# A fused attention and MLP kernel: 64-row matmuls made 128 rows high, transposes in other PSUM banks, weight blocks requested earlier

## The chip, the cores and the metric

The kernel runs on one core of a Trainium2 chip. The metric is the device time of one execution, in microseconds (us).

## What is computed

Three parts follow each other. Batch is 4, heads 8, sequence 576, head dimension 64, 128 features, model width 512.

```python
def _attn_ref(q, k, v, w_phi):            # (4, 8, 576, 64), w_phi (64, 128)
    def phi(x):
        proj = np.einsum('bhsd,df->bhsf', x, w_phi)
        proj = proj - np.max(np.abs(proj), axis=-1, keepdims=True)
        return np.concatenate([np.exp(proj), np.exp(-proj)], axis=-1)
    q_p, k_p = (phi(q), phi(k))
    kv = np.einsum('bhsf,bhsd->bhfd', k_p, v)
    z = np.sum(k_p, axis=2)
    num = np.einsum('bhsf,bhfd->bhsd', q_p, kv)
    den = np.einsum('bhsf,bhf->bhs', q_p, z)[..., None] + 1e-06
    return num / den
def _moe_ref(x, w_ch1, w_ch2):            # x (4, 576, 512), w_ch1 (512, 2048), w_ch2 (2048, 512)
    u = x + np.real(np.fft.fft(np.fft.fft(x, axis=1), axis=2))
    un = layer_norm(u)
    return u + np.maximum(un @ w_ch1, 0.0) @ w_ch2
def _moe2_ref(x, g_ln, w_ch1, w_ch2):
    return x + np.maximum((layer_norm(x) * g_ln) @ w_ch1, 0.0) @ w_ch2
```

`layer_norm` stands for the mean and variance over the last axis written out in the reference. The MLP weights come in double precision and the kernel makes single-precision numbers of them.

## The kernel before

**First stage: attention and DFT, to about 320 us.** The 32 heads are worked in 16 units of two heads. 576 tokens are four tiles of 128 and a rest of 64. The rest of q and the rest of k share one tile, "mix": q in rows 0 to 63, k in rows 64 to 127. For each unit `project` (L116) multiplies the tiles with w_phi (pp, in PSUM), VectorE takes the largest magnitude (mx) and subtracts it (pm). `k_exp` (L134) has ScalarE make both exponentials of k (ek); for mix it takes rows 64 to 127 alone. `kv` (L143) sums over keys (pk): five tiles, two heads, two signs, each matmul in two instructions; the last tile uses rows 64 to 127 alone (L148). `q_exp` (L160) transposes the q tiles on TensorE, the four full ones into pt (named ptq in the profile), the 64 rows of mix into ptc (L162), and ScalarE makes the exponentials eq from both (L168, L169). `num` (L172) multiplies eq with the sums z (px), and VectorE divides (L188 to L201). The DFT of the real attention output is done by symmetry: `fold` (L206) adds or subtracts mirrored halves, `seq_stage` (L233) transforms along the sequence (pb), `dim_stage` (L271) along the model width (pd). A last matmul in `dim_stage` (L285) takes the rows nyq, four of them used, times alt, a row of alternating signs; both are 64 rows high.

**PSUM.** All banks come from three tags (L48): p has two banks and holds pp, ptc and in the second stage ph; t has two for pt and ptx; n has four for pk, px, pb, pd and acc.

**Second stage: the two MLPs.** Weights come in 64 blocks of 512 KB, eight to a group of 512 hidden columns. `fetch` (L314) requests one block (wraw) on the queue of SyncE into one of two raw buffers (`RAW = 2`, L28); `to_float` (L329 to L343) makes single precision of it on ScalarE and VectorE (wm), with the last read of the raw buffer at L342; `decode` (L345) calls `fetch` and `to_float` and splits the result into a high and a low part (wh, wl). `mm1` (L418) makes ph and from it hh and hl on ScalarE and VectorE, `mm2` (L436) makes acc, and VectorE adds it to the result.

**Order.** The program order is written out: `rounds` (L559) for the units, `pieces` (L527) for decode and DFT steps of a round, `side` (L478) for steps between `mm1` and `mm2`. The framework then works out the order on each engine by its own timeline simulation (L657). Decode steps stand in rounds 2 to 17 for the first group (L532) and at fixed places of the group before for the others (L493 to L498):

```python
        for k in range(8):
            side.setdefault((0, 2 + k // 4, 2 * (k % 4)), []).append(partial(decode, 0, 1, k))
        for p in range(1, 7):
            for k in range(8):
                at = (p, k // 2, 1 + 4 * (k % 2))
                side.setdefault(at, []).append(partial(decode, (p + 1) // 4, (p + 1) % 4, k))
```

Of the kernel before, what the change touches and what calls it, by code (L numbers as in the profile page):

```python
# [10 lines left out]
F32 = mybir.dt.float32  # L11
F32R = mybir.dt.float32r
I32 = mybir.dt.int32
U32 = mybir.dt.uint32
AF = mybir.ActivationFunctionType
# [3 lines left out]
B, H, S, D = 4, 8, 576, 64  # L19
F = 128  # L20
DM = H * D
NE = DM // 2 + 2
# [9 lines left out]
def fused_kernel(ctx, tc, qk_c, v_c, w_phi, w1s, w2s, g_ln, cs_c, cd_c, perm_c, out):  # L32
    nc = tc.nc
    P = 128
# [7 lines left out]
    dpool = dft_stack.enter_context(tc.tile_pool(name="dft", bufs=1))  # L42
    att_stack = ExitStack()
    apool = att_stack.enter_context(tc.tile_pool(name="atk", bufs=1, side="right"))
    bpool = att_stack.enter_context(tc.tile_pool(name="atq", bufs=1))

    def ps_tile(tag, shape, name):
        return psum.tile(shape, F32, tag=tag, bufs={"p": 2, "t": 2, "n": 4}[tag], name=name)  # L48
# [5 lines left out]
    ident = perm  # L54
# [5 lines left out]

    cs = dpool.tile([P, 3, 2, 2, NS], F32R, name="cs")
    cd = dpool.tile([P, 2, 2, 2, NE], F32R, name="cd")
    alt = dpool.tile([64, NE], F32R, name="alt")
    wbd = apool.tile([P, 2, F], F32, name="wbd")

    def load_consts():
# [7 lines left out]
    def load_dft_consts():  # L74
        nc.sync.dma_start(perm, perm_c)
        for x, c in ((cs, cs_c), (cd, cd_c[0:P])):
            x = x.rearrange("p a b c e -> p (a b c e)")
            follow(x[:, 0:1], 0)
            nc.gpsimd.dma_start(x, c)
        nc.gpsimd.dma_start(alt, cd_c[P : P + 64, 0:NE])  # L80

    def late_consts():
        nc.sync.dma_start(gcol, g_ln.rearrange("(k p) -> p k", p=P))
# [12 lines left out]
    st = [dict() for _ in range(NUNIT)]  # L96
# [19 lines left out]
    def project(u, name):  # L116
# [14 lines left out]
        nc.vector.tensor_tensor(out=t, in0=pp, in1=mx.unsqueeze(2).to_broadcast([P, 2 * n, F]), op=ALU.subtract)  # L131
        st[u]["pm", name] = t

    def k_exp(u, name):  # L134
        t = st[u]["pm", name]
        n = 1 if name == "mix" else 2
        r = slice(64, P) if name == "mix" else slice(0, P)
        e = apool.tile([P, 2 * n, 2, F], F32, tag=f"ek{n}", bufs=2, name="ek")
        for sgn in range(2):
            nc.scalar.activation(e[r, :, sgn], t[r], AF.Exp, scale=1.0 - 2.0 * sgn)  # L140
        st[u]["ek", name] = e

    def kv(u):  # L143
        pk = ps_tile("n", [P, 4, D + 1], "pk")
        first = True
        for t in range(5):
            e = st[u]["ek", ("k0", "k1", "mix")[t // 2]]
            r = slice(64, P) if t == 4 else slice(0, P)  # L148
            for j in range(2):
                for sgn in range(2):  # L150
                    nc.tensor.matmul(  # L151
                        pk[:, 2 * j + sgn, :], e[r, 2 * (t % 2) + j, sgn], st[u]["v"][r, t, j],
                        start=first, stop=(t == 4), skip_group_check=True,
                    )
                    first = False
        z = bpool.tile([P, 4, D + 1], F32, tag="z", bufs=2, name="z")
        nc.scalar.copy(z, pk)
        st[u]["z"] = z

    def q_exp(u, j):  # L160
        ptc = ps_tile("p", [P, 64], "ptc")
        nc.tensor.transpose(ptc, st[u]["pm", "mix"][0:64, j, :], ident[0:64, 0:64])  # L162
        pt = ps_tile("t", [P, 4, P], "ptq")
        for t in range(4):
            nc.tensor.transpose(pt[:, t, :], st[u]["pm", f"q{t // 2}"][:, 2 * (t % 2) + j, :], ident)  # L165
        e = bpool.tile([P, 2, S], F32, tag="eq", bufs=2, name="eq")
        for sgn in range(2):
            nc.scalar.activation(e[:, sgn, 512:S], ptc, AF.Exp, scale=1.0 - 2.0 * sgn)  # L168
            nc.scalar.activation(e[:, sgn, 0:512], pt.rearrange("p t s -> p (t s)"), AF.Exp, scale=1.0 - 2.0 * sgn)  # L169
        st[u]["eq", j] = e  # L170

# [59 lines left out]
    nyq = []  # L231

    def seq_stage(b, w):  # L233
        xs = dst[b].pop(("x", w))
        bh = dpool.tile([P, 2, 2 * P], F32R, tag="bh", bufs=2, name="bh")
        bl = dpool.tile([P, 2, 2 * P], F32R, tag="bl", bufs=2, name="bl")
        if b % 2 == 0:
            mixed[w] = [dpool.tile([P, 2, P], F32R, tag=f"b{x}{w}", bufs=1, name=f"b{x}{w}") for x in "pq"]
        ch, cl = mixed[w]
        if w == 0:  # L240
            if not nyq:
                nyq.append(dpool.tile([64, 3 * P], F32R, name="nyq"))
                nc.vector.memset(f32(nyq[0]), 0.0)
        r = slice(64 * (b % 2), 64 * (b % 2) + 64)
        for m in range(3 - w):
            pb = ps_tile("n", [P if m < 2 else 2, NS], "pb")
            mm = []
            for kk in range(3):
                for cc in range(2):
                    if m < 2:  # L250
                        c = slice(m * P, (m + 1) * P)
                        mm.append((pb, xs[:, kk, c], cs[:, kk, w, cc]))
                        if kk < 2 and cc == 0:
                            mm.append((pb, xs[:, 3 + kk, c], cs[:, kk, w, cc]))
                    elif kk < 2:
                        mm.append((pb, xs[:, kk : kk + 4 : 3, 256], cs[:, kk, w, cc]))
                    else:
                        mm.append((pb[0:1], xs[:, kk, 256:257], cs[:, kk, w, cc]))
            for n, (o, a, c) in enumerate(mm):
                nc.tensor.matmul(o, a, c, start=(n == 0), stop=(n == len(mm) - 1), skip_group_check=(m == 2))  # L260
            if m < 2:
                parts = ((bh[:, m], bl[:, m]), (ch[:, m, r], cl[:, m, r]))
            else:
                rc = slice(2 * P + r.start, 2 * P + r.stop)
                parts = [(nyq[0][0:2, x], nyq[0][32:34, x]) for x in (slice(0, 2 * P), rc)]
            for (oh, ol), src in zip(parts, (pb[:, 0 : 2 * P], pb[:, 2 * P : NS])):
                nc.scalar.copy(oh, src)
                nc.vector.tensor_tensor(out=ol, in0=src, in1=f32(oh), op=ALU.subtract)
        dst[b]["b", w] = (bh, bl)
# [31 lines left out]


    weights = {}
    wpools = {}

    def group_tiles(layer, g):
# [7 lines left out]
    def fetch(layer, g, n):  # L314
        w, i = divmod(n, 4)
        src = w1s[layer] if w == 0 else w2s[layer]
        r = slice(i * P, (i + 1) * P) if w == 0 else slice(g * 512 + i * P, g * 512 + (i + 1) * P)
        c = slice(g * 1024, (g + 1) * 1024) if w == 0 else slice(0, 1024)
        raw = wpool.tile([P, WB, 2], I32, tag="wraw", bufs=RAW, name="wraw")
        if layer == 0 and g == 0 and n < RAW:  # L320
            follow(f32(raw[:, 0, 0:1]), 1)
        nc.sync.dma_start(raw.rearrange("p f t -> p (f t)"), src.bitcast(I32)[r, c])
        return raw

    def to_float(raw):

# [18 lines left out]
    def decode(layer, g, n):  # L345
        if n == 0:
            group_tiles(layer, g)
        w, i = divmod(n, 4)
        wh, wl = weights[layer, g][w]
        raw = fetch(layer, g, n)  # L350
        m = to_float(raw)
        if layer == 1 and w == 0:

            nc.scalar.activation(wh[:, i], f32(m), AF.Copy, scale=gcol[:, i : i + 1])
            nc.vector.scalar_tensor_tensor(
                out=wl[:, i], in0=f32(m), scalar=gcol[:, i : i + 1], in1=f32(wh[:, i]),
                op0=ALU.mult, op1=ALU.subtract,
            )
        else:
            nc.scalar.copy(wh[:, i], f32(m))  # L360
            nc.vector.tensor_tensor(out=wl[:, i], in0=f32(m), in1=f32(wh[:, i]), op=ALU.subtract)
# [112 lines left out]
    def moe(last_dft):  # L474
# [3 lines left out]
        side = {}  # L478
# [11 lines left out]
        side.setdefault((0, 1, 2), []).append(partial(prepare, 0, 2))  # L490
        side.setdefault((0, 1, 7), []).append(partial(prepare, 0, 3))
        side.setdefault((0, 2, 7), []).append(partial(prepare, 0, 4))
        for k in range(8):  # L493
            side.setdefault((0, 2 + k // 4, 2 * (k % 4)), []).append(partial(decode, 0, 1, k))
        for p in range(1, 7):
            for k in range(8):
                at = (p, k // 2, 1 + 4 * (k % 2))
                side.setdefault(at, []).append(partial(decode, (p + 1) // 4, (p + 1) % 4, k))  # L498

        for layer, g, c in steps:  # L500
            p = 4 * layer + g
# [15 lines left out]


    nc.vector.memset(ub[0][:, 0], 0.0)
    warm = ps_tile("n", [P, DM], "warm")  # L520
    for n in range(2):
        nc.tensor.matmul(warm, ub[0][:, 0, 0:P], ub[0][:, 0], start=True, stop=True)
# [4 lines left out]
    def at(step, f, *a):  # L527
        pieces.setdefault(step, []).append((f, a))

    wpools[0] = wpool  # L530
    xpools[0] = xpool
    for n, step in enumerate((2, 3, 4, 7, 8, 11, 15, 17)):  # L532
        at(step, decode, 0, 0, n)
    at(9, prepare_norm, 0)
    at(12, prepare_tiles, 0, 0, (0, 1))
# [28 lines left out]
    for i in range(NUNIT + 2):  # L564
        for name, ahead in rounds:
            u = i + ahead
# [27 lines left out]
def _constants():  # L594
# [7 lines left out]
    e = np.arange(NE)  # L602
    ang = 2 * np.pi * ((d[:, :, None] * e[None, None, :]) % DM) / DM
    live = (e <= DM // 2).astype(np.float64)
    cd = np.stack([np.stack(_split(f(ang) * live), axis=2) for f in (np.cos, np.sin)], axis=1)
    cd = cd.reshape(128, -1)
    last = np.zeros((64, cd.shape[1]), np.float32)
    last[[0, 1, 32, 33], :NE] = np.where(e % 2 == 0, 1.0, -1.0) * live
    perm = np.eye(128, dtype=np.float32)
    return (  # L610
# [54 lines left out]
```

## Time and profile before

| | |
|---|---|
| median of 3 runs | 1109.78 us (1109.66 to 1110.68) |
| the profiled execution, in all | 1109.95 us |
| its span, first to last instruction | 1108.2 us |
| granted TensorE clock, mean share | 0.994 |
| TensorE (PE) busy | 1086.3 us |
| weight loads (PEld) busy | 927.9 us |
| VectorE (DVE) busy | 615.0 us |
| ScalarE (ACT) busy | 340.5 us |
| GpSimd (POOL) busy | 45.3 us |

Busy time of an engine is the time in which at least one of its instructions runs. Matmuls are pipelined and overlap: one starts before the one ahead has ended, so the spacing of their starts tells more than their durations. In the rows a shape such as 64*128 64x65 is rows*columns of the weights in the array, then partitions x elements of the moving operand. In a timeline row the first number is the start of a merged group in us, the second its length from the first start to the last end, xN the number of instructions, and what stands in brackets is the idle time of the engine before it and what ended it.

### The profile page before, as it was taken

How to read it: one execution, taken by the hardware profiler on the slowest of the kernel's cores; microseconds unless marked ns; L12 is line 12 of the kernel's file. 1: busy time of each engine (PE TensorE's matmuls, PEld its weight loads, DVE VectorE, ACT ScalarE, POOL GpSimd, SP SyncE). 2: the span in 40 equal slices, each digit the busy share in tenths (PEclk: the TensorE clock that was granted, in tenths of full speed). 3: DMA queues.
4: the chain of work that ended last, by engine and by line, in shares of the span. 5: the costliest groups of instructions: out<-in, count | busy, mean ns of one | idle time of the engine just before them, and what ended most of it. 6: DMA issues, size and time to landing. Idle time of an engine off the chain costs nothing.

```text
span 1108.2 us, 14381 instructions
## 1 busy us (share of the span) xinstructions
PE 1086.3 (98%) x5806; PEld 927.9 (84%) x5806; DVE 615.0 (55%) x1315; ACT 340.5 (31%) x682; POOL 45.3 (4%) x53
## 2 busy tenths in 40 slices
PE   9899999999999999999999999999999999999996
PEld 7789989999788888888888788888878888888885
DVE  5897586774879476238327755762383264222131
ACT  4545454454435131113113343521231132011110
POOL 1000020300210000000000000000000000000010
PEclk9899999999999999999999999999999999999998
DMA  7452121110003122003101300220031011000111
GB/s 257 144 161 77 46 60 42 57 46 1 1 1 114 39 76 76 1 1 114 39 1 50 103 1 1 64 89 1 1 115 38 1 39 38 1 1 10 48 48 67
DMA packets 19755, 57.26 MB, mean 52 GB/s; under 512 B 2728, under 2 KB 3432, under 8 KB 19432
## 3 DMA queue, kind: packets, MB, share of 16 engines
q1 hardware_dynamic: 18536, 51.01, 14.3%
q0 software_dynamic: 1008, 5.19, 1.3%
q8 instruction: 46, 0.75, 0.3%
q14 instruction: 21, 0.17, 0.1%
q10 hardware_dynamic: 144, 0.13, 0.0%
HBM read 51.60 MB, written 4.72 MB: 51 GB/s over the span
## 4 chain that ended last, share of the span: by engine, by line
PE 86%; DVE 8%; DMA 4%; ACT 2%; issue 1%; POOLq 0%; POOL 0%; DVEq 0%; SPq 0%; ACTq 0%
PE acc L443 33%; PE ph L427 32%; PE pk L151 5%; PE px L181 5%; PE pp L121 5%; DMA wraw<-in_moe_w_ch 4%; PE pb L260 2%; PE ptq L165 1%; PE ptx L409 1%; PE pd L287 1%; DVE wm L342 1%; DVE wm L337 1%; DVE xx L215 1%; DVE wm L334 0%; DVE hl L431 0%
## 5 line engine op out<-in xcount | busy, mean ns | idle before, releaser
L427 PE MATMUL ph<-xth,wh 128*128 128x512 f32 (+1 forms) x640 | 236.2, 369 | 0.7 <-ACT xth L411 0.7
L427 PE MATMUL ph<-xtl,wh 128*128 128x512 f32 (+1 forms) x640 | 235.8, 368 | 0.0
L427 PE MATMUL ph<-xth,wl 128*128 128x512 f32 (+1 forms) x640 | 235.7, 368 | 0.0
L431 DVE SCALAR_TENSOR_TENSOR hl<-ph,hh 128x512 fp32r<-128x512 f32 (+1 forms) x160 | 101.5, 634 | 232.7 <-ACT hh L430 232.4
L430 ACT ACTIVATE hh<-ph 128x512 fp32r<-128x512 f32 (+1 forms) x160 | 88.4, 554 | 461.6 <-PE ph L427 456.4
L443 PE MATMUL acc<-wl,hh 128*128 128x512 f32 x576 | 224.2, 390 | 0.0
L443 PE MATMUL acc<-wh,hh 128*128 128x512 f32 x576 | 221.2, 391 | 2.5 <-ACT hh L430 2.5
L443 PE MATMUL acc<-wh,hl 128*128 128x512 f32 x576 | 195.3, 390 | 0.0
L427 PEld LDWEIGHTS ph<-xth,wh 128*128 128x128 f32 x640 | 120.4, 188 | 21.8 <-ACT xth L411 0.9
L427 PEld LDWEIGHTS ph<-xtl,wh 128*128 128x128 f32 x640 | 120.5, 188 | 20.7
L427 PEld LDWEIGHTS ph<-xth,wl 128*128 128x128 f32 x640 | 120.6, 188 | 20.0
L445 DVE TENSOR_TENSOR u<-acc,u 128x512 f32<-128x512 f32 x128 | 81.2, 682 | 94.3 <-PE acc L443 94.1
L443 PEld LDWEIGHTS acc<-wh,hh 128*128 128x128 f32 x576 | 108.1, 188 | 25.4 <-ACT hh L430 3.6
L443 PEld LDWEIGHTS acc<-wl,hh 128*128 128x128 f32 x576 | 108.2, 188 | 22.1
L443 PEld LDWEIGHTS acc<-wh,hl 128*128 128x128 f32 x576 | 107.1, 188 | 21.2
L121 PE MATMUL pp<-wbd,qk 128*128 128x256 f32 x288 | 80.2, 398 | 3.2 <-ACT eq L168 1.9
L151 PEld LDWEIGHTS pk<-vv,ek 128*128 128x128 f32 (+1 forms) x640 | 77.6, 191 | 5.2 <-ACT ek L140 1.8
L151 PE MATMUL pk<-vv,ek 128*128 128x65 f32 (+1 forms) x640 | 80.1, 273 | 0.8 <-ACT ek L140 0.6
L181 PEld LDWEIGHTS px<-z,eq 128*128 128x128 f32 (+1 forms) x640 | 76.3, 186 | 3.9 <-issue 0.3
L181 PE MATMUL px<-z,eq 128*128 128x65 f32 (+1 forms) x640 | 76.1, 268 | 0.0
L125 DVE TENSOR_REDUCE mx<-pp 128x4 f32<-128x512 f32 (+1 forms) x80 | 50.5, 631 | 45.5 <-PE pp L121 44.8
L140 ACT ACTIVATE ek<-pm 128x512 f32<-128x512 f32 (+1 forms) x96 | 48.2, 551 | 44.5 <-DVE pm L131 44.2
(100 smaller groups left out, 954.2 us busy)
## 6 DMA issues: line engine op xcount, KB each, us to landing
wraw<-in_moe_w_ch SPq DMA_DIRECT2D x64, 512.0 KB
vv<-in_v SPq DMA_DIRECT2D x16, 325.0 KB
qk<-in_qk SPq DMA_DIRECT2D x15, 320.0 KB
qk<-in_qk SPq DMA_DIRECT2D x16, 256.0 KB
out<-u SPq DMA_DIRECT2D x8, 256.0 KB
cs<-c_seq POOLq DMA_DIRECT2D x1, 1920.0 KB, 10.3
cd<-c_dim POOLq DMA_DIRECT2D x1, 1032.0 KB, 13.0
out<-uc SPq DMA_DIRECT2D x4, 126.0 KB
```

The source lines that it names most:

```text
L121: nc.tensor.matmul(pp[:, 2 * i : 2 * i + 2, :], qk[:, KT[name] + i], wbd.rearrange("p h f -> p (h f)"), start=True, stop=True)
L125: nc.vector.tensor_reduce(out=mx, in_=pp, op=ALU.max, axis=AX.X, apply_absolute_value=True)
L140: nc.scalar.activation(e[r, :, sgn], t[r], AF.Exp, scale=1.0 - 2.0 * sgn)
L151: nc.tensor.matmul(pk[:, 2 * j + sgn, :], e[r, 2 * (t % 2) + j, sgn], st[u]["v"][r, t, j], start=first, stop=(t == 4), skip_group_check=True,)
L165: nc.tensor.transpose(pt[:, t, :], st[u]["pm", f"q{t // 2}"][:, 2 * (t % 2) + j, :], ident)
L181: nc.tensor.matmul(px[0 : c.stop - c.start, t, :], e[:, sgn, c], z[:, 2 * j + sgn], start=(t == 0 and sgn == 0), stop=(sgn == 1), skip_gro ...
L260: nc.tensor.matmul(o, a, c, start=(n == 0), stop=(n == len(mm) - 1), skip_group_check=(m == 2))
L427: nc.tensor.matmul(ph[:, 0:n], a[:, kk, sl], x[:, kk], start=(i == 0), stop=(i == 11))
L430: nc.scalar.activation(hh[:, 0:n], ph[:, 0:n], AF.Relu)
L431: nc.vector.scalar_tensor_tensor(out=hl[:, 0:n], in0=ph[:, 0:n], scalar=0.0, in1=f32(hh[:, 0:n]), op0=ALU.max, op1=ALU.subtract)
L443: nc.tensor.matmul(acc, x[:, sl], w[:, f], start=(f == 0 and n == 0), stop=(f == 3 and n == 2))
L445: nc.vector.tensor_tensor(out=x, in0=acc, in1=x, op=ALU.add)
```

## The change

The 64-row operands become 128 rows high. The exponentials of mix go into two lasting tiles whose upper half is set to zero once; the last tile of `kv` then takes all 128 rows (v has zeros there, and ones in the column of the sums, which the zero exponentials cancel). ptc transposes all of mix, and 64 of its columns are read as before. alt and nyq get 64 more rows of zeros. ptc moves from tag p to tag n. `fetch` leaves `decode` and becomes a step of its own: in the first group one round ahead of its decode, in the others in the place of the decode before it, ahead of that decode.

```diff
-    alt = dpool.tile([64, NE], F32R, name="alt")
+    alt = dpool.tile([P, NE], F32R, name="alt")
...
-        nc.gpsimd.dma_start(alt, cd_c[P : P + 64, 0:NE])
+        nc.gpsimd.dma_start(alt, cd_c[P : 2 * P, 0:NE])
...
+    ekm = [apool.tile([P, 2, 2, F], F32, name=f"ekm{i}") for i in range(2)]
+
     def k_exp(u, name):
         t = st[u]["pm", name]
         n = 1 if name == "mix" else 2
         r = slice(64, P) if name == "mix" else slice(0, P)
-        e = apool.tile([P, 2 * n, 2, F], F32, tag=f"ek{n}", bufs=2, name="ek")
+        if name == "mix":
+            e = ekm[u % 2]
+        else:
+            e = apool.tile([P, 2 * n, 2, F], F32, tag="ek", bufs=2, name="ek")
...
-            r = slice(64, P) if t == 4 else slice(0, P)
...
-                        pk[:, 2 * j + sgn, :], e[r, 2 * (t % 2) + j, sgn], st[u]["v"][r, t, j],
+                        pk[:, 2 * j + sgn, :], e[:, 2 * (t % 2) + j, sgn], st[u]["v"][:, t, j],
...
     def q_exp(u, j):
-        ptc = ps_tile("p", [P, 64], "ptc")
-        nc.tensor.transpose(ptc, st[u]["pm", "mix"][0:64, j, :], ident[0:64, 0:64])
+        ptc = ps_tile("n", [P, P], "ptc")
+        nc.tensor.transpose(ptc, st[u]["pm", "mix"][:, j, :], ident)
...
-            nc.scalar.activation(e[:, sgn, 512:S], ptc, AF.Exp, scale=1.0 - 2.0 * sgn)
+            nc.scalar.activation(e[:, sgn, 512:S], ptc[:, 0:64], AF.Exp, scale=1.0 - 2.0 * sgn)
...
-                nyq.append(dpool.tile([64, 3 * P], F32R, name="nyq"))
+                nyq.append(dpool.tile([P, 3 * P], F32R, name="nyq"))
...
-        return raw
+        raws[layer, g, n] = raw
...
-        raw = fetch(layer, g, n)
+        raw = raws.pop((layer, g, n))
...
-        for k in range(8):
-            side.setdefault((0, 2 + k // 4, 2 * (k % 4)), []).append(partial(decode, 0, 1, k))
-        for p in range(1, 7):
-            for k in range(8):
-                at = (p, k // 2, 1 + 4 * (k % 2))
-                side.setdefault(at, []).append(partial(decode, (p + 1) // 4, (p + 1) % 4, k))
+        def weight_steps(p, times):
+
+            blocks = [((p // 4, p % 4, k), t) for k, t in enumerate(times)]
+            side.setdefault(blocks[0][1], []).insert(0, partial(fetch, *blocks[0][0]))
+            for (a, t), nxt in zip(blocks, blocks[1:] + [None]):
+                side[t] = side.get(t, []) + ([partial(fetch, *nxt[0])] if nxt else []) + [partial(decode, *a)]
+
+        weight_steps(1, [(0, 2 + k // 4, 2 * (k % 4)) for k in range(8)])
+        for p in range(2, 8):
+            weight_steps(p, [(p - 1, k // 2, 1 + 4 * (k % 2)) for k in range(8)])
...
+    for e in ekm:
+        nc.gpsimd.memset(e[0:64], 0.0)
...
     for n, step in enumerate((2, 3, 4, 7, 8, 11, 15, 17)):
+        at(step - 1, fetch, 0, 0, n)
         at(step, decode, 0, 0, n)
...
-    last = np.zeros((64, cd.shape[1]), np.float32)
+    last = np.zeros((128, cd.shape[1]), np.float32)
```

## Rows read from the trace of the kernel before

**Rows 1.** The page, busy time and share of the span.
```profile
PE 1086.3 (98%) x5806; PEld 927.9 (84%) x5806; DVE 615.0 (55%) x1315; ACT 340.5 (31%) x682; POOL 45.3 (4%) x53
```

**Rows 2.** Stretches: length, PE, PEld, DVE, ACT, POOL busy, PEclk, DMA share, GB/s.
```profile
20.00:100.00 80.00, 75.71 (x537) 68.17 (x536) 69.96 (x174) 41.41 (x96) 5.01 (x2) 0.96 0.42 137
40.00:60.00 20.00, 17.56 (x115) 15.66 (x114) 17.82 (x47) 10.31 (x23) 0.00 (x0) 0.83 0.40 131
```

**Rows 3.** Groups of TensorE by shape: busy us, mean ns, idle before.
```profile
L151 PE MATMUL pk<-vv,ek 64*128 64x65 f32 x128 | 18.1, 279 | 0.0
L162 PE MATMUL ptc<-perm,pm 64*128 64x64 f32 x32 | 8.7, 272 | 2.4 <-ACT eq L168 2.0
L287 PE MATMUL pd<-alt,nyq 64*128 64x258 f32 x10 | 3.8, 382 | 0.0
```

**Rows 4.** Timeline of TensorE, 186 to 204 us, full-height work.
```profile
193.92 2.12 PE L151 MATMUL pk<-vv,ek 128*128 128x65 f32 x18
...
200.73 0.60 PE L409 MATMUL ptx<-perm,un 128*128 128x128 f32 x4
```

**Rows 5.** Timeline of TensorE, 94 to 97 us.
```profile
94.39 0.44 PE L165 MATMUL ptq<-perm,pm 128*128 128x128 f32 x2
94.75 1.10 PE L151 MATMUL pk<-vv,ek 64*128 64x65 f32 x8
95.79 0.44 PE L165 MATMUL ptq<-perm,pm 128*128 128x128 f32 x2
96.16 0.27 PE L162 MATMUL ptc<-perm,pm 64*128 64x64 f32 x1
96.36 0.66 PE L165 MATMUL ptq<-perm,pm 128*128 128x128 f32 x4
96.85 0.38 PE L121 MATMUL pp<-wbd,qk 128*128 128x256 f32 x1
```

**Rows 6.** Timeline of TensorE, 198 to 201 us.
```profile
198.19 0.44 PE L165 MATMUL ptq<-perm,pm 128*128 128x128 f32 x2
198.56 0.54 PE L151 MATMUL pk<-vv,ek 64*128 64x65 f32 x3
198.84 0.27 PE L162 MATMUL ptc<-perm,pm 64*128 64x64 f32 x1
...
199.86 1.03 PE L121 MATMUL pp<-wbd,qk 128*128 128x256 f32 x4
```

**Rows 7.** Timeline of TensorE, 138 to 139 us.
```profile
138.07 0.28 PE L287 MATMUL pd<-cd,bh 128*128 128x258 f32 x1
138.29 0.38 PE L287 MATMUL pd<-alt,nyq 64*128 64x258 f32 x1
138.60 0.39 PE L287 MATMUL pd<-cd,bh 128*128 128x258 f32 x1
...
138.94 0.40 PE L287 MATMUL pd<-cd,bh 128*128 128x258 f32 x2
```

**Rows 8.** Timeline of TensorE, 64 to 66 us.
```profile
64.52 0.65 PE L165 MATMUL ptq<-perm,pm 128*128 128x128 f32 x4
...
66.00 0.70 PE L121 MATMUL pp<-wbd,qk 128*128 128x256 f32 x2 [0.43 <-ACT eq L168]
```

**Rows 9.** Timeline of all engines, 44 to 53 us.
```profile
45.98 0.68 ACT L329 ACTIVATE wm<-wraw 128x512 f32<-128x512 f32 x1 [3.08 <-DVE uc L201]
...
47.74 0.37 PE L162 MATMUL ptc<-perm,pm 64*128 64x64 f32 x1 [2.01 <-ACT eq L168]
...
48.53 2.08 PE L121 MATMUL pp<-wbd,qk 128*128 128x256 f32 x4 [0.43 <-ACT eq L168]
```

**Rows 10.** Waits of the DMA queue of SyncE: us in total, times, longest.
```profile
SPq L322 <- DVE wm L342: 694.4, 62, 96.5
```

**Rows 11.** Waits of TensorE: us in total, times, longest.
```profile
PE acc L443 <- ACT hh L430: 2.5, 2, 1.4
```

**Rows 12.** GpSimd: a group by line, and its timeline from 0 to 13 us.
```profile
L211 POOL TENSOR_TENSOR xe<-u 128x1024 f32<-128x1024 f32 x8 | 19.3, 2409 | 232.1 <-DVE u L195 223.2 <-DVE xx L219 9.0
...
7.01 0.18 POOL L72 CAST cs<-mx 128x1 fp32r<-128x1 f32 x1 [4.26 <-DVE mx L125]
```

More of the change, by code (lines that the diff above doesn't have):

```diff
@@ L303, in fused_kernel @@
     weights = {}
+    raws = {}
     wpools = {}
```

## The prediction

> **What bounds the kernel now.** First the page's busy times [rows 1]: TensorE has matmuls in flight for 98% of the span, so only what changes its own stream can shorten the run; but "busy" hides how densely the matmuls start. Second, the table by stretches [rows 2]: from 20 to 100 us TensorE is idle for 4.3 us, 2.4 of them between 40 and 60, where its granted clock is 0.83 on average; VectorE is busy for 70 of those 80 us. Third, the groups of TensorE by shape [rows 3]: the change touches the three that use only 64 rows of the array: 128 matmuls pk, 32 transposes ptc, 10 matmuls of alt with nyq. Their own durations look harmless. Fourth, the timeline of TensorE alone, where the distance from start to start shows what durations hide.
>
> **What a 64-row instruction costs.** Undisturbed, eighteen full pk take 2.12 us, one every (2.12 - 0.27)/17 = 0.11; four full transposes ptx take 0.60, one every 0.11 [rows 4]. Four patterns with 64 rows come up between 13 and 322 us:
> - A ptc alone among full-height work. The second ptq of 95.79 starts at 95.79 + 0.44 - 0.27 = 95.96, ptc at 96.16, the next ptq at 96.36, pp at 96.85 [rows 5]. That is 0.89 us for six transposes worth 6 x 0.11 = 0.65: 0.24 lost, about 0.09 on the way in, 0.09 on the way out and 0.06 behind it.
> - Eight pk of 64 rows without a ptc: from 94.39 + 0.44 - 0.27 = 94.56 to 95.96 is 1.40 for ten instructions worth 1.11: 0.29 lost [rows 5].
> - pk of 64 rows with a ptc among them: from 198.19 + 0.17 = 198.36 to 199.86 is 1.50 for twelve instructions worth 1.32: 0.18 lost [rows 6].
> - An alt matmul: bh to alt is 0.22, alt to bh 0.31, the next two 0.34 together; 0.87 for four worth 4 x 0.12 (the two bh at 138.94 are 0.40 - 0.28 apart): 0.38 lost [rows 7].
>
> The third pattern is where a rule speaks against the change. Row: the ptc at 198.84 starts 0.01 us after the third pk of its group (198.56 + 0.54 - 0.27 = 198.83), so it costs nothing there [rows 6]; made full height it takes its 0.11. That is why 0.18 stands there and not 0.29. The Trainium skill, TensorE: Matmul & The Clock Gate, section "Part 3: Packing small matmuls", says it in general: matmuls whose row groups differ can run side by side in the array, which full height gives up. By the rule every ptc beside such a pk loses by the change; without it the sum below would be 1.5 us larger (14 x 0.11).
>
> **The change, part by part.**
> 1. Full height for pk, ptc and alt. In the timeline I count 17 ptc alone, 14 groups of pk with a ptc among them, 4 groups without, and 10 alt (one of them with the last ptc right behind it), which accounts for all 32 ptc and 10 alt [rows 3]. With every instruction at its full-height spacing, 17 x 0.24 + 14 x 0.18 + 4 x 0.29 + 10 x 0.38 = 4.1 + 2.5 + 1.2 + 3.8 = **11.6 us** go from the engine that sets the end. The px with 64 columns keep their shape, and what that costs.
> 2. ptc moved from the two p banks to the four n banks. In three rounds pp, which also needs a p bank, waits until ScalarE has read ptc. One of them: the last ptq starts at 64.52 + 0.65 - 0.27 = 64.90, pp at 66.00 [rows 8]; undisturbed the way from ptq over ptc to pp is 0.40, so 0.70 is lost, and 3 x 0.70 = **2.1 us** in all. I take it as saved: pp then shares its banks with nobody. In place of it ptc may wait for an n bank, with all later work of TensorE behind it (third rival).
> 3. The fourth such place, from 45 to 49 us, has ptc idle for 2.01 and pp for 0.43, and after it the clock is at half for a while [rows 9]: 0.83 over 20 us [rows 2] is 3.4 us at the lower level, so 1.7 us of work lost. Together 4.1. But ScalarE is what is late: it sat 3.08 us before the decode step at 45.98, with the exponentials behind it [rows 9], and the following ptq and px wait for those whatever bank ptc has. Bounds 0 and 4.1. With p free one group of four pp can go ahead, 4 x 0.22 = **0.9** ((1.03 - 0.38)/3 in rows 6), which I take.
> 4. Requests for raw blocks one round ahead. The DMA queue waited 694 us, 62 times, for VectorE's last read of an earlier block [rows 10]: with two raw buffers a request already goes out when a buffer comes free, and asking earlier frees none. **0**. Bounds: a gain of 2.5, if TensorE's two waits for hh, which follow ScalarE's waits for late blocks, went [rows 11]; a loss of as much if two more came up. Behind a request that stands earlier in the queue and waits, the loads of q, k and v queue; they are made two units ahead, so a wait shorter than a round is hidden.
> 5. Side work. Two GpSimd memsets of 64x512: from about nothing to twice the fold's 2.4 us [rows 12]. GpSimd sits 4.26 us before its first constant request anyway [rows 12], so the requests leave at most 0.5 us late, and seq_stage reads those constants several rounds later. The alt constant doubles to 129 KB and is first read at 138 us [rows 7]. The nyq memset keeps its columns and comes before VectorE has other work. All 0. ScalarE still reads 64 columns of ptc.
>
> Sum: 11.6 + 2.1 + 0.9 = 14.6. The profiled execution took 1109.95 us (span 1108.2 and what lies around it), 0.17 above the median of the runs: 1109.95 - 14.6 = **1095.3 us**.
>
> **Rivals.**
> - *VectorE keeps the early part.* It is busy for 70 of 80 us from 20 to 100 [rows 2], since weight decoding is squeezed in there. If nothing won in that stretch stays (6 lone ptc 1.4, 4 groups of pk with a ptc 0.7, one without 0.3, and the 3.0 of points 2 and 3), 9.2 is left: 1100.8. For: the share. Against: TensorE's idle time in rows 8 and 9 is put down to ScalarE.
> - *Everything goes:* the whole 4.1 of point 3 and the 2.5 of point 4, so 14.6 + 3.2 + 2.5 = 20.3: 1089.7. Against: rows 10.
> - *The n banks become the bound (slower).* pk, px, pb, pd, acc and ptc would share four banks, and TensorE works in order. If every ptc waited 0.70 for its bank, as pp does now for its own, 32 x 0.70 = 22.4 would be added to a gain of 14.6: 1117.8. It decides from 14.6/32 = 0.46 us per ptc. Against: n has twice as many banks as p, and gets only two more users a unit.
> - *A new stall.* The order of all instructions is worked out anew when the program is built (line 657); one more place like that of 45 us costs 4.1: 1099.4, beside the first rival.
> - *The fetch order does nothing* is my forecast for that part, not a rival.
>
> **Numbers.** Forecast (1091.5 to 1098.5) 0.55; VectorE or a new stall keeps part (to 1106) 0.25; everything goes (below 1091.5) 0.13; no difference 0.04; n banks, slower, 0.03. The range leaves out the ends of the second and third case and the last two: 1089 to 1104. A measurement of this kernel can tell about 0.2% (2.2 us) from no change: faster 0.93, same 0.04, slower 0.03.
>
> **What would show it.** By shape, no row of pk, ptc or alt has 64 rows; in the timeline ptq, ptc and ptq follow at 0.11 us, bh, alt and bh at 0.12, and no ptc starts 0.01 behind a pk. No pp waits for eq of line 168. The queue's wait for VectorE stays near 694 us, and the second stage, from the last px to the end, keeps its length. The prediction is wrong if full-height spacing is not 0.11, if ptc, pk or px wait for a bank, or if the first 100 us are as long as now.

## The result and the profile after

The changed kernel takes 1124.95 us (median of 4 runs, 1122.67 to 1127.48) beside 1109.72 us for the kernel before (4 runs): a ratio of 1.0137, 95% interval 1.0116 to 1.0158. It is slower by 15 us; forecast were 14.6 us less. Times and ratios here and below leave out the executions that ran in a slower state (two of e3, one of e14, and some of the kernel before beside them). The profiled execution took 1125.57 us, with a span of 1123.8.

The page after, busy time and granted clock in 40 slices, answers to [rows 1]:

```profile
PE 1094.9 (97%) x5806; PEld 941.9 (84%) x5806; DVE 615.6 (55%) x1315; ACT 338.6 (30%) x682; POOL 44.5 (4%) x55
...
PEclk9889989979999999999999999999999999999998
```

TensorE is busy for longer, not for less. The digits 7 and 8 of the clock in the first nine slices (28 us each) say why: for part of them the array ran at the lower of its two levels, 1.2 and 2.4 GHz. The clock of the whole execution was 0.994 before:

```profile
core 0: 1123.8 us, clock 0.976
```

By shape, the three groups of [rows 3] are full height, and the timeline shows them at the spacing forecast: ptq, ptq, ptc, ptq, ptq, pp from 50.44 to 50.99 is 0.55 us for five transposes, 0.11 each; bh, alt, bh is 0.13 and 0.11.

```profile
L156 PE MATMUL pk<-vv,ekm 128*128 128x65 f32 x128 | 19.3, 289 | 0.0
L167 PE MATMUL ptc<-perm,pm 128*128 128x128 f32 x32 | 9.2, 288 | 0.0
L292 PE MATMUL pd<-alt,nyq 128*128 128x258 f32 x10 | 2.8, 281 | 0.0
```

```profile
50.44 0.39 PE L170 MATMUL ptq<-perm,pm 128*128 128x128 f32 x2
50.66 0.27 PE L167 MATMUL ptc<-perm,pm 128*128 128x128 f32 x1
50.77 0.38 PE L170 MATMUL ptq<-perm,pm 128*128 128x128 f32 x2
50.99 1.03 PE L121 MATMUL pp<-wbd,qk 128*128 128x256 f32 x4
...
145.44 0.28 PE L292 MATMUL pd<-cd,bh 128*128 128x258 f32 x1
145.57 0.28 PE L292 MATMUL pd<-alt,nyq 128*128 128x258 f32 x1
145.68 0.29 PE L292 MATMUL pd<-cd,bh 128*128 128x258 f32 x1
```

So the switching between heights is gone. What came in its place stands in the table by stretches (columns as in [rows 2]). First the stretch of the kernel before that [rows 2] lack, then the kernel after:

```profile
100.00:320.00 220.00, 217.23 (x1519) 196.51 (x1519) 155.77 (x383) 102.34 (x244) 28.42 (x23) 1.00 0.11 35
```

```profile
20.00:100.00 80.00, 73.95 (x474) 66.79 (x475) 68.38 (x170) 37.35 (x86) 4.70 (x2) 0.87 0.39 125
100.00:320.00 220.00, 211.91 (x1488) 197.60 (x1488) 147.77 (x360) 100.47 (x242) 23.91 (x19) 0.94 0.12 39
...
36.00:45.00 9.00, 9.00 (x37) 7.90 (x37) 5.16 (x17) 4.04 (x8) 0.00 (x0) 0.50 0.24 90
63.00:72.00 9.00, 9.00 (x45) 9.00 (x45) 7.04 (x14) 2.25 (x6) 0.00 (x0) 0.50 0.70 212
163.00:171.00 8.00, 8.00 (x30) 6.94 (x31) 4.30 (x23) 3.45 (x6) 0.00 (x0) 0.50 0.00 1
231.00:243.00 12.00, 12.00 (x53) 11.33 (x52) 7.03 (x20) 3.84 (x9) 1.19 (x2) 0.50 0.09 28
```

From 20 to 320 us TensorE is idle for 6.05 + 8.09 = 14.1 us, where it was 4.29 + 2.77 = 7.1. And there are four stretches in which it is busy all the time, with nothing to wait for, at half clock (PEclk 0.50), and a fifth of 3.4 us from 312 us on. The waits of TensorE name whom it waits for (us in total, times, longest); then the queue of [rows 10]:

```profile
PE pp L121 <- DVE pm L131: 5.4, 6, 2.2
PE pk L156 <- DVE rr L298: 3.0, 2, 2.2
...
PE pb L265 <- DVE xs L231: 1.8, 1, 1.8
...
PE px L186 <- ACT eq L174: 1.5, 2, 1.3
```

```profile
SPq L328 <- DVE wm L348: 681.1, 60, 97.3
```

In the kernel before, TensorE waited for eq by way of ptc and pp [rows 8, 9], and of the first three waits it had 0.3 us in all (pb for xs). One of the places, TensorE and then VectorE ahead of it:

```profile
57.80 1.56 PE L121 MATMUL pp<-wbd,qk 128*128 128x256 f32 x6
61.53 1.13 PE L121 MATMUL pp<-wbd,qk 128*128 128x256 f32 x4 [2.17 <-DVE pm L131]
```

```profile
58.89 0.67 DVE L343 SCALAR_TENSOR_TENSOR wm<-wraw,wm 128x512 int32<-128x512 int32 x1
59.49 0.41 DVE L200 TENSOR_TENSOR u<-px,rd 128x256 f32<-128x256 f32 x1
...
60.47 0.68 DVE L125 TENSOR_REDUCE mx<-pp 128x4 f32<-128x512 f32 x1
61.07 0.41 DVE L131 TENSOR_TENSOR pm<-pp,mx 128x256 f32<-128x256 f32 x1
```

pp needs a bank that pm has read. VectorE has no idle time in these rows; it is simply late with pm, because decode and division stand ahead of it. 1.2 us after pp gets going, at 62.7 us, the clock falls to half, and it stays there until 73.

**A balance of the runs.** For a profiled execution I take three numbers: TensorE's idle time from 20 to 320 us (stretch minus busy), the loss by the clock (span times one minus the mean clock; 0.0005 of rounding is 0.6 us), and what is left of the difference to the kernel before. e12 to e15 are not in it, since their extra matmuls would stand in the rest.

| | profiled, us | to before | idle | clock loss | rest |
|---|---|---|---|---|---|
| before | 1109.95 | | 7.1 | 6.6 | |
| after | 1125.57 | +15.6 | +7.1 | +20.3 | -11.8 |
| e1 | 1108.68 | -1.3 | +3.2 | +5.5 | -10.0 |
| e2 | 1121.81 | +11.9 | +6.5 | +16.9 | -11.5 |
| e3 | 1115.85 | +5.9 | +3.2 | +1.1 | +1.6 |
| e4 | 1105.58 | -4.4 | +1.4 | -1.1 | -4.7 |
| e5 | 1115.19 | +5.2 | +6.2 | +8.9 | -9.9 |
| e6 | 1181.19 | +71.2 | +24.9 | +55.9 | -9.5 |
| e7 | 1118.88 | +8.9 | +7.1 | +10.1 | -8.3 |
| e8 | 1106.05 | -3.9 | +3.3 | +2.2 | -9.4 |
| e9 | 1109.73 | -0.2 | +4.1 | +5.5 | -9.8 |
| e10 | 1108.45 | -1.5 | +2.7 | +7.7 | -11.9 |
| e11 | 1104.18 | -5.8 | -0.5 | +4.4 | -9.7 |

The rest is in the main what the density of the stream gives: nothing with 64-row work (e3), -4.7 with ptc alone left at 64 rows (e4), -8 to -12 wherever all is full height. It also holds whatever else differs, such as a second stage that is 1.8 us shorter in the changed kernel. There the gain was won, and then lost to waits and, three times as much, to the clock. More than half of that loss lies behind 100 us: 5.3 of the 7.1 us of waits, and by the clock about 13 us (0.06 of 220, before 0.00) beside 7 us ahead of it (0.13 of 80, before 0.04).

### The profile page after: what moved, and what is told of

It reads as the page before. It is cut to its first block, busy times and chain, and to the rows that moved or that the text cites. A ratio compares the mean times of both kernels' runs of the same rounds, so it can differ in the third digit from the quotient of the medians.

```text
span 1123.8 us, 14370 instructions
## 1 busy us (share of the span) xinstructions
PE 1094.9 (97%) x5806; PEld 941.9 (84%) x5806; DVE 615.6 (55%) x1315; ACT 338.6 (30%) x682; POOL 44.5 (4%) x55
## 4 chain that ended last, share of the span: by engine, by line
PE 84%; DVE 9%; DMA 4%; ACT 1%; issue 1%; POOLq 0%; SPq 0%; POOL 0%; DVEq 0%; ACTq 0%
PE acc L449 32%; PE ph L433 32%; PE px L186 5%; PE pk L156 5%; PE pp L121 4%; DMA wraw<-in_moe_w_ch 4%; PE pb L265 2%; PE ptx L415 1%; DVE wm L343 1%; DVE wm L348 1%; DVE mx L125 1%; DVE pm L131 1%; PE ptq L170 1%; DVE u L302 1%; DVE xx L220 1%
## 5 line engine op out<-in xcount | busy, mean ns | idle before, releaser
L186 PEld LDWEIGHTS px<-z,eq 128*128 128x128 f32 (+1 forms) x640 | 79.1, 198 | 7.1 <-ACT eq L174 2.7
L186 PE MATMUL px<-z,eq 128*128 128x65 f32 (+1 forms) x640 | 80.7, 283 | 2.3 <-ACT eq L174 1.5
L156 PE MATMUL pk<-vv,ek 128*128 128x65 f32 x512 | 67.5, 291 | 3.0 <-DVE rr L298 3.0
L156 PEld LDWEIGHTS pk<-vv,ek 128*128 128x128 f32 x512 | 66.6, 210 | 4.5 <-DVE rr L298 3.6
L121 PEld LDWEIGHTS pp<-wbd,qk 128*128 128x128 f32 x288 | 53.6, 203 | 17.0 <-DVE pm L131 5.3
## 6 DMA issues: line engine op xcount, KB each, us to landing
cd<-c_dim POOLq DMA_DIRECT2D x1, 1032.0 KB, 13.1
```

The costliest lines, as they stand in the source:

```text
L121: nc.tensor.matmul(pp[:, 2 * i : 2 * i + 2, :], qk[:, KT[name] + i], wbd.rearrange("p h f -> p (h f)"), start=True, stop=True)
L156: nc.tensor.matmul(pk[:, 2 * j + sgn, :], e[:, 2 * (t % 2) + j, sgn], st[u]["v"][:, t, j], start=first, stop=(t == 4), skip_group_check=True,)
L186: nc.tensor.matmul(px[0 : c.stop - c.start, t, :], e[:, sgn, c], z[:, 2 * j + sgn], start=(t == 0 and sgn == 0), stop=(sgn == 1), skip_gro ...
```

## The experiments

The framework works the order out anew for every program. On TensorE, VectorE and ScalarE, compared place by place, earlier requests alone change no place of the order, full height of pk and alt none, full height of ptc 26 of TensorE's 5,023, and the move of ptc to tag n some 680 (counted by the names of the tiles that are read and written). So the move of the bank is also a change of the order, and most runs below tell these two apart. Times are medians; beside these runs the kernel before had medians of 1108.5 to 1109.4 us.

**e1 to e4: the parts.**

```diff
 e1  full height for pk, ptc, alt as in the change, but
+        ptc = ps_tile("p", [P, P], "ptc")            # requests as before
 e2  e1, but
+        ptc = ps_tile("n", [P, P], "ptc")
 e3  the kernel before, but
+        ptc = ps_tile("n", [P, 64], "ptc")
 e4  pk and alt full height, ptc as before
```

e1: 

> Full height for pk, ptc and alt, ptc left in the p banks, requests as before. The order of instructions is almost that of the kernel before (26 of 5,023 places differ on TensorE, 35 of 1,318 on VectorE). Theory A (the bank move is the harm, by a new order of instructions): the 11.6 us of the prediction come in, about 1098 us, and the waits of pp for eq stay. Theory B (a denser stream of matmuls runs into VectorE and drops the clock): 1115 to 1125 us with several spells at the lower clock. Theory C (the earlier requests are the harm): about 1098 us.

e2: 

> The change without the earlier requests. Its order on every engine is that of the changed kernel, place by place. Theories A and B: the changed kernel's time, 1123 to 1127 us, since the requests decide nothing. Theory C: about 1098 us.

e3: 

> ptc in the n banks alone, 64 rows high as before. Theory A: slower than the changed kernel, about 1125 + 11.6 = 1136 us, since the stalls of the new order stay and the 64-row losses come back. Theory B: about as before or a little faster, 1106 to 1110 us. Theory C: 1106 to 1110 us.

e4: 

> Full height for pk and alt only, ptc as before; the order on every engine is exactly that of the kernel before. Theory A by the prediction's patterns: the 10 alt give 3.8; groups of pk no longer switch shape, but each of 32 ptc now stands alone among full-height work and costs 0.24, so pk gives 14 x (0.18 - 0.24) + 4 x 0.29 = 0.3; about 1106 us. Theory B: 1110 us or more.

e1 took 1106.03 (ratio 0.997, 0.9954 to 0.9985), e2 1121.88 (1.0113, 1.0096 to 1.013), e3 1116.3 (1.0054, 1.0028 to 1.0081), e4 1106.14 (0.9986, 0.9975 to 0.9997). Full height is worth 3 us; the bank costs 6 to 7 alone and 16 on top of full height. Theory C (the requests) is out: e2 has none of them. Neither of the others holds as it was written: A is right for e4 and nearly for e2, and has e1 8 us too low and e3 20 too high; B has e1 at least 9 us too high and e3 at least 6 too low. The bank is the larger harm, but it is worse in a denser stream. The stretches of e1:

```profile
20.00:100.00 80.00, 74.69 (x544) 68.02 (x543) 69.84 (x174) 42.11 (x96) 5.02 (x2) 0.98 0.42 137
100.00:320.00 220.00, 215.01 (x1509) 199.39 (x1508) 155.31 (x381) 100.36 (x242) 28.39 (x23) 0.97 0.11 35
```

5.3 + 5.0 us idle and a clock below 1: even without the bank move, most of the 10 us won is given back in this execution, and about 7 of the 10 by the medians.

**e5, e6, e9: bank and order apart.** The order of one kernel is fixed in another by order-only edges along each engine. Banks of one tag go to tiles in program order (233 of 233 tiles of tag n do in the kernel before). There pk runs ahead of ptc in 15 of the 16 units (unit 12 is the other), while the program has e0, which makes ptc, ahead of kv; with ptc in n every pk has to come behind it. So for the old order in the new bank kv must stand first.

```diff
 e5, e6, e9
+    for a, b in zip(seq, seq[1:]):                    # seq: order of the other kernel
+        tc.add_manual_dep(ins[b], ins[a].name, NoSync, reason="order")
 e5, e7, e9 (list of a round)
-        ("dft", 0), ("e0", 0), ("kv", 0), ("e1", 0),
+        ("dft", 0), ("kv", 0), ("e0", 0), ("e1", 0),
 e9 (in dim_stage, after the first pd)
+            if (b, m, w) == (1, 2, 0):
+                q_exp(12, 0)
```

e5: 

> Full height for pk, ptc and alt, ptc in the n banks, requests as before, and the order on every engine held at that of e1_high by order-only edges (one ptc stands behind a pd instead of ahead of it; for that kv stands ahead of e0 in the program). Theory O (the harm is the new order: banks of a tag are given out in program order, so with ptc in n every pk has to come behind the first ptc of its unit, where it ran ahead of it before): the bank alone costs nothing, 1102 to 1107 us, the waits of pp for pm and of pk for rr at most 2 us together, clock 0.99. Theory K (the harm is that five kinds of tile share four n banks): 1116 to 1122 us, pk, px or ptc waiting for a bank.

e6: 

> The reverse: full height, ptc in the p banks as before, and the order on every engine held at that of e2_highbank (12 matmuls of pp stand behind a ptc, since p banks go in program order too). Theory O: 1117 to 1124 us, with pp waiting for DVE's pm for 4 us or more in all and spells at half clock behind the stalls, as in e2_highbank. Theory K: no fifth user in the n banks, so 1103 to 1108 us, as e1_high.

e9: 

> As e5, but without its one misplaced ptc: e0 of unit 12 stands in the program between the two pd of its round, so that ptc takes its n bank ahead of the last pd, and the order on all engines is that of e1_high place by place. Only the bank differs. Theory O2 (banks go in program order, and what that does to the order is the whole harm; in e5 one ptc waited 2.5 us behind a pd for rr, with 10.2 us at half clock behind it): 1102 to 1107 us, no wait for rr. Theory K2 (the n bank costs something by itself even in the old order): 1110 to 1116 us, as e5, with other waits in the place of that one.

e5 took 1114.39 (1108.24 to 1120.75), ratio 1.0046 (1.0017 to 1.0074): between the two theories. Its one misplaced ptc did wait:

```profile
218.42 0.43 PE L166 MATMUL ptc<-perm,pm 128*128 128x128 f32 x1 [2.47 <-DVE rr L297]
```

e9, without it and with e1's order place by place, took 1112.15 (1107.62 to 1115.39), 1.0031 (1.0012 to 1.005). That is as K2 had it: the bank costs something in the old order too, and other waits come in the place of that one. But no tile waits long for an n bank (ptc once, 0.5 us for rr), so K's reason is out. The largest wait of e9:

```profile
PE ptq L170 <- DVE pm L132: 5.5, 4, 2.2
```

The timeline of TensorE in e9, then the same place in e1, then the clock of e9 behind it:

```profile
46.98 1.03 PE L122 MATMUL pp<-wbd,qk 128*128 128x256 f32 x4
50.20 0.66 PE L170 MATMUL ptq<-perm,pm 128*128 128x128 f32 x4 [2.19 <-DVE pm L132]
...
52.60 3.78 PE L186 MATMUL px<-z,eq 128*128 128x65 f32 x26 [0.88 <-ACT eq L174]
```

```profile
47.66 0.33 PE L166 MATMUL ptc<-perm,pm 128*128 128x128 f32 x1 [0.42 <-ACT eq L172]
48.41 1.13 PE L121 MATMUL pp<-wbd,qk 128*128 128x256 f32 x4 [0.43 <-ACT eq L172]
...
52.37 3.89 PE L185 MATMUL px<-z,eq 128*128 128x65 f32 x30 [1.52 <-ACT eq L173]
```

```profile
55.00:66.00 11.00, 11.00 (x51) 10.15 (x50) 7.19 (x24) 4.35 (x9) 0.00 (x0) 0.53 0.32 97
```

With p free, pp starts at 46.98 and not at 48.41, as point 3 had it, and then TensorE stands for 2.19 + 0.88 = 3.1 us, where it had stood for 0.42 + 0.43 + 1.52 = 2.4. I read the short waits of ptc and pp as a brake ahead of a VectorE that is late anyway; without it the same delay comes in one piece, with half clock after it, where e1 has PEclk 1.00 from 45 to 70 us. This is one place in one execution each. Over the 300 us e9's profiled execution is idle for only 0.9 us more than e1's, at the same clock. The 6 us between the medians lie mostly in the clock: 0.983 to 0.992 in e9's ten executions, 0.989 to 0.995 in e1's.

So the 16 us between e1 and e2 have two parts, by the medians: 6 for the bank in the old order (e1 to e9), 10 for the order that the framework makes of it (e9 to e2).

e6 took 1180.39 (1.0627, 1.0582 to 1.0672), 56 us over what O gave it. So it can't price the new order by itself: that order, with 12 pp moved to fit the p banks, brings waits of its own there. TensorE waits for VectorE's pm eleven times, and 55.9 of the 71.2 us in the balance are lost by the clock.

```profile
PE pp L121 <- DVE pm L131: 11.7, 6, 3.5
PE ptc L166 <- DVE pm L131: 9.0, 5, 3.8
```

**e7: is it pk behind ptc?** The line of the list above alone, on e2.

> One line beside e2_highbank: in the list of a round kv stands ahead of e0, ptc in the n banks, the order worked out by the framework. Theory O: pk runs ahead of ptc again and the time falls to 1102 to 1110 us. Theory K: 1117 to 1123 us. If it is not pk behind ptc but the rest of the new order (pp in pairs ahead of px, now that p holds pp alone) that leaves TensorE to VectorE: 1112 to 1118 us.

1120.06 (1.0105, 1.0088 to 1.0121): no. pk runs ahead again, and the waits are elsewhere, for both engines:

```profile
PE px L185 <- ACT eq L173: 5.1, 3, 2.1
PE ptq L169 <- DVE pm L131: 3.3, 2, 1.9
PE pp L121 <- DVE pm L131: 2.9, 2, 2.4
```

So theory O falls in its first form. Which single place of the new order does the harm has no answer; each order worked out with ptc in n (after, e2, e3, e7) has TensorE idle for over 1 us at five or six places from 20 to 320 us, where the kernel before has one.

**e8: the requests.** `fetch` of the change, on e1; the order is the same.

> e1_high (full height, ptc in p) with the raw blocks requested one round ahead; the order on every engine is that of e1_high. Forecast of the prediction for this part, nothing: 1103 to 1109 us, the queue's wait for VectorE 670 to 700 us. Theory F (the requests are what separates the changed kernel, 1125, from e2_highbank, 1122): 1107 to 1112 us, 3 us above e1_high, with more of ScalarE's waits for wraw or of TensorE's for hh.

1105.66 (0.9974, 0.996 to 0.9989), e1 has 1106.03; the queue's wait for VectorE is 690.6 us in e8 and 691.0 in e1. The requests do nothing in e1's order. The 3 us between e2 and the changed kernel, whose orders are equal too, are not settled: the intervals of their ratios overlap.

**e10, e11: is it VectorE?** Order held, VectorE given less to do; half of the DFT sum and the low words of eight weight blocks are left out.

```diff
+        nc.vector.tensor_scalar(out=low[:, c], ...)   # c: 1 column, 8 blocks
+        nc.vector.tensor_tensor(out=m[:, c], ...)
...
-                out=x[:, 257:512], in0=x[:, 257:512], in1=rr[:, 1 - f, 255:0:-1], op=ALU.add
+                out=x[:, 257:258], in0=x[:, 257:258], in1=rr[:, 1 - f, 255:256], op=ALU.add
```

e10: 

> The changed kernel with its order held on every engine, and VectorE relieved in the first stage: the last two steps of to_float work on 1 of 512 columns for the first eight weight blocks, and the mirrored add at the end of dim_stage on 1 of 255 columns for all batches (so the low words of those weights and half of the DFT sum are left out). About 1 us less per block and 0.4 to 2.6 us less per add; nothing less on TensorE. Theory V (TensorE waits 1 to 2.3 us at a few places for a VectorE that is late, and each such wait is followed by a spell at half clock): the waits of pp for pm and of pk for rr fall from 8.4 to under 3 us, at most two spells stay, 1103 to 1112 us. Rival W (the waits are for banks and places in the order, not for VectorE's speed, or the clock falls whatever the waits): 1118 to 1126 us.

e11: 

> The same relief in e1_high with its order held. Theory V: there VectorE is waited for 2.6 us only (pm), and one or two spells follow; 1098 to 1104 us, 3 to 7 us below e1_high, so that the distance between the changed kernel and e1_high (19 us) shrinks to under 10 us when both are relieved. Rival W: the distance stays 15 to 20 us.

e10, the changed kernel relieved, took 1108.63 (0.9997, 0.9985 to 1.0009): 16 us less, with nothing taken from TensorE. e11, e1 relieved, took 1103.07 (0.9932, 0.9903 to 0.9961): 3 us less. The distance of the two fell from 19 to 5.6 us. The waits that are left in e10:

```profile
PE px L186 <- ACT z L162: 2.8, 1, 2.8
PE pk L156 <- DVE rr L298: 2.6, 2, 1.8
...
PE pp L121 <- DVE pm L131: 2.2, 1, 2.2
```

The waits for pm and rr fell from 8.4 to 4.8 us, not under 3; two stretches at half clock are left (68.5 to 79 and 218.5 to 229 us), and the time came out as V had it. A late VectorE is the cause. The 16 us are far more than the waits that went: in the balance 4.4 us are idle time and 12.6 the clock. What was taken from VectorE includes the last read of eight raw buffers, so blocks can also come earlier; the runs don't part the two.

**e12 to e15: the waits or the clock?** Order held, VectorE and ScalarE untouched, and extra matmuls in the places where TensorE stood idle.

```diff
+    def fill(n, o=None):
+        o = ps_tile("t", [P, P], "idle") if o is None else o
+        for _ in range(n):
+            nc.tensor.matmul(o, perm, perm, start=True, stop=True, skip_group_check=True)
```

e12: 

> The changed kernel with its order held on every engine, and TensorE kept busy at four of the places where it stood idle in the profile: 12, 20, 14 and 6 extra 128-column matmuls of the unit matrix by itself (0.11 us each, results overwritten or not read) stand ahead of px of unit 1 (34.02 us, idle 1.28), pp of unit 3 (61.53, 2.17), pp of unit 9 (158.76, 1.51) and px of unit 8 (160.12, 0.68). VectorE and ScalarE do what they did. Theory S (the spells at half clock come of the idle time, and they, not the waits, are most of the loss): the three spells behind those places (35.4, 62.7 and 161.7 us, 10.2 us each) do not come, those at 230 and 312 stay; about 12 to 15 us less, 1109 to 1114 us, with VectorE as late as before. Rival W (the waits themselves are the loss, or the spells come whatever TensorE does in them): 1122 to 1128 us.

e14: 

> e12 with half as many extra matmuls (6, 10, 7, 3): each took 0.22 us, not 0.11, so that e12 put 11.3 us of extra work on TensorE where it had stood idle for 5.6. Theory S: the same three spells stay away, and the 5.7 us of extra work go: 1112 to 1118 us. Rival W: the extra work was hidden behind the waits and nothing comes back, 1119 to 1123 us; or the waits that are left bring the spells back, 1120 to 1126 us.

e13: 

> The same in e1_high with its order held: 8 extra matmuls ahead of px of unit 2 (52.37 us, idle 1.5) and 10 ahead of pp of unit 9 (153.00, idle 1.12). Theory S: the spell behind 153 us (13.7 us in the profiled run, in about half of its runs by the two clusters of times) does not come, so all runs lie near the faster cluster, 1102 to 1105 us, clock 0.992 or more. Rival W: 1104 to 1109 us, in two clusters as e1_high.

e15: 

> e13 with 5 instead of 10 extra matmuls ahead of pp of unit 9, where TensorE had stood idle for 1.12 us (5 take 1.1). Theory S: as e13 or up to 1.1 us less, 1101 to 1104 us, all runs at a clock of 0.992 or more. Rival W: two clusters as in e1_high, 1104 to 1108 us.

e12 took 1120.99 (1.0122, 1.0068 to 1.0175), 4 us less and not the 12 of S: too much was put in, since each extra matmul runs as two of 0.11 us. e14, with half of it, took 1115.4 (1.0054, 1.0037 to 1.0071), 9.5 us under the changed kernel, as S had it. Its stretches behind the filled places, the last with the end of a spell at half clock that began at 149.5; then the place that was at 61 us, now at 57:

```profile
31.00:50.00 19.00, 18.96 (x142) 17.32 (x140) 17.90 (x45) 11.45 (x27) 0.00 (x0) 1.00 0.53 167
57.00:68.00 11.00, 8.72 (x66) 7.82 (x65) 9.36 (x20) 3.88 (x9) 0.00 (x0) 1.00 0.52 168
155.00:165.00 10.00, 10.00 (x73) 9.19 (x73) 7.74 (x33) 5.97 (x13) 0.00 (x0) 0.92 0.13 36
```

```profile
55.05 2.39 PE L103 MATMUL idle<-perm 128*128 128x128 f32 x20
57.70 1.13 PE L130 MATMUL pp<-wbd,qk 128*128 128x256 f32 x4 [0.26 <-DVE pm L140]
```

pp still waits for pm until 57.70, but the clock stays at 1.00 behind it. All three spells at which the filling was aimed are gone, in e12 too. In their place e14 has two new ones: from 71 us, behind a new wait of px for z of 3.6 us, and from 149.5, behind one of pk for rr of 0.8 that the changed kernel has too, there with no spell; the one behind pk's other wait for rr (224.8 us) stays. So the spells come of TensorE's idle time and not of VectorE's lateness as such, and they cost more than the waits do.

e13 took 1103.07 (1101.82 to 1105.22; 0.9938, 0.9919 to 0.9957) with all six runs at a clock of 0.995 or more; e1's ten lie in two clusters, 1102.7 to 1104.4 at 0.993 to 0.995 and 1107.6 to 1109.2 at 0.989 to 0.990. e15 took 1105.12 (0.9948, 0.9919 to 0.9976): above S's range and inside W's, though at the clock that S gave it (0.992 to 0.997). So e13 speaks for S, and e15 leaves it open. Both beat the kernel before by their intervals, and e13 has the lowest median of the versions that leave nothing out.

## Why the prediction was wrong

**Point 1, full height, 11.6 us: right as a price, wrong as a sum.** The spacing is 0.11 and 0.12 as forecast, and the balance has 11.8 for the changed kernel and 10.0 for e1. It was then booked in full as time. Point 1 took TensorE's stream as all that sets the end, although [rows 2] had VectorE busy for 70 of 80 us; of the 10.0 us of e1's profiled execution, which lies in the slower of its two clusters, 3.2 came back as waits and 5.5 by the clock. The rival "VectorE keeps the early part" had the cause, but not the place or the size: 2.2 of e1's 3.2 us of waits and its longest stretch at half clock lie behind 100 us, where VectorE is busy for 71% of the time, and the rival let the gain be lost, and not more. The page rule of the Trainium skill that spoke against point 1 (TensorE: Matmul & The Clock Gate, "Part 3: Packing small matmuls") was weighed rightly: with the overlap of ptc taken off the price was 11.6, without it 13.1, and the balance has 8 to 12.

**Point 2, ptc to the n banks, 2.1 us: this step failed.** "I take it as saved: pp then shares its banks with nobody." pp doesn't wait for eq of ptc any more, as said. But the step didn't ask what is late next, and put no price on the order that comes with the bank. In place of 2.1 us saved, the move costs 16 by the medians of e1 and e2. Of their profiled executions, 13.1 us apart, the balance puts 3.3 down to waits, 11.4 to the clock and -1.5 to the rest. e9, where nothing but the bank differs from e1, is 6 us slower, and ptq waits 5.5 us for pm.

**Point 3, 0.9 us: the same failure.** The group of pp did go ahead (46.98), and the wait grew from 2.4 to 3.1 us. The clock is also read wrongly there: 0.83 over 20 us is 6.8 us at half clock (PEclk is 0.50 from 46.3 to 53.1 us) and 3.4 us lost, twice the 3.4 and 1.7 of the prediction, so a place like this costs 5.8 us and not 4.1.

**The order.** The prediction knew that the order is worked out anew, priced one stall at 4.1 us against a gain, and gave slower 0.03. The changed kernel has five places of 1.3 to 2.2 us (34.0, 61.5, 158.8 with 160.1, 230.4, 310.7). In waits and clock they cost 7.1 + 20.3 = 27.4 us, about 5.5 each. So even 4.1 was too little for one, and the number of them was not bounded from above; the order could have been compared before the time was forecast.

**Points 4 and 5: right.** e8 has the requests at nothing, and the second stage keeps its length: from the last px to the last matmul 819.4 us before and 817.6 after.

**The rival that was slower** had the n banks fill up, each ptc waiting 0.70. The side was right, the mechanism mostly wrong: ptc waits for no bank in the kernel after. pk does, twice, 3.0 us in all: rr is VectorE's read of pd, which gives the n bank back. That is one of the prediction's own signs of being wrong, but a small part of 27.4 us.

## What to carry to other kernels

Where a framework works out the order, a tile that gets another bank gets the whole kernel another order: compare the orders first, and price the bank by the waits at new places, not by the wait that goes. A short wait taken from ahead of an engine that is fed by a late one can gather into a longer wait, and a wait of 1 to 2 us of TensorE must be priced with the time at half clock that can follow. If such a wait can't be avoided, work that nobody needs can be cheaper than none (e13, e14).

## What was unexpected

The same wait at the same place, in the same order, once brings half clock and once not. Timeline and stretch of e1, then of e8, which differs in its requests alone:

```profile
153.00 0.67 PE L121 MATMUL pp<-wbd,qk 128*128 128x256 f32 x2 [1.12 <-DVE pm L131]
```

```profile
155.00:168.00 13.00, 13.00 (x54) 12.19 (x54) 5.46 (x21) 6.92 (x15) 0.00 (x0) 0.50 0.24 73
```

```profile
155.35 0.67 PE L121 MATMUL pp<-wbd,qk 128*128 128x256 f32 x2 [1.13 <-DVE pm L131]
```

```profile
157.00:170.00 13.00, 12.05 (x89) 11.01 (x89) 8.82 (x31) 9.73 (x20) 0.00 (x0) 1.00 0.25 73
```

1.12 and 1.13 us of idle time; in the next 13 us 54 matmuls at 1.2 GHz in the one, 89 at 2.4 GHz in the other. Nor does half clock follow every wait elsewhere: in e10 pp waits 2.2 us for pm at 56.4 us, and the clock is 1.00 from 56 to 60; e3 is idle for 1.1 to 1.8 us at six places, with half clock behind the first alone. This would make e1's two clusters of times, but that is not shown: only the slower one has a profile. One execution of such a kernel doesn't tell its time. The Trainium skill, TensorE: Matmul & The Clock Gate, section "A second HAM failure mode: psum-queue depth-cycling", has it that a TensorE that idles briefly between groups of matmuls while banks go round can make its clock swing between the two levels. The trace agrees that the clock swings so, and adds that one wait of 1 to 2 us can stand ahead of it, and that a TensorE busy for 97% of the span lost 20 us more by the clock than the kernel before. What decides whether a wait brings it was not tried.

That nearly the same order costs 1180 us in one bank and 1122 us in another (e6, e2) was not expected either. With e9 it suggests that an order is good only with the banks that it was worked out for.
